# An attention and gMLP kernel whose planner hands the VectorE/GpSimd port to the engine that waits, with squares pushed to GpSimd, part of a layer norm offered to ScalarE, and the last stores on two queues

## Chip, cores, metric

One core of one Trainium2 chip. The metric is device microseconds (us) of one execution. A run reads about 1.8 us more than the span from the first to the last instruction in its trace, so spans are compared with spans and times with times. Single executions of this kernel scatter by a few us (291.0 to 296.7 for the kernel before), which is why differences under about 1% are told with an interval.

Engine names in the profile: PE is TensorE's matmul, PEld its weight load, DVE is VectorE, ACT is ScalarE, POOL is GpSimd, SP is SyncE (the q behind a name is its DMA queue). L441 is line 441 of that kernel; lines shift between kernels, so L418 of before is L441 of after.

## The reference

```python
def rmsnorm(x, g):
    rms = np.sqrt(np.mean(x * x, axis=-1, keepdims=True) + 1e-06)
    return x / rms * g
q_n, k_n = rmsnorm(q, g_q), rmsnorm(k, g_k)          # q, k, v: 8 x 12 x 448 x 64
scores = 1 / 8 * np.matmul(q_n, k_n.transpose(0, 1, 3, 2))
attn = softmax(scores); x = attn @ v                 # then heads side by side: 8 x 448 x 768

h = np.maximum(x @ w_in, 0.0)                        # 768 -> 1024
u, v = h[..., :512], h[..., 512:]
v_n = (v - mean(v)) / np.sqrt(var(v) + 1e-06)        # the layer norm of the change
v_s = einsum('ts,bsd->btd', w_spatial, v_n) + b_spatial[None, :, None]
out = (u * v_s) @ w_out                              # 8 x 448 x 768
```

The heads are worked off in 24 groups of 4 (three groups for each of the 8 batch entries). "Group 2 ended" means that the first batch entry's attention is complete; from then on its unit (the gMLP part) can start.

## The kernel before

The program is not written in the order in which it runs. Each piece of work is a `Task` with the engines that may do it and what each would cost; a `Planner` simulates the engines while the kernel is built, and emits each instruction at the place that this simulation gives it. The chip gets the resulting instruction lists, one for each engine. Between the lists there are semaphores for data and for buffers only.

VectorE and GpSimd share one port pair into the on-chip memory SBUF (the prediction names the page of the Trainium skill and a case in this trace: a GpSimd scaling of 2.58 us in place of 1.69). The planner models it with `locked`, a time up to which the port is taken:

```python
    def start_of(self, t, e, free):
        at = max(free[e], t.after)
        if e == "POOL" or (e == "DVE" and t.port):
            at = max(at, self.locked)          # wait for the port, in the plan
        ...
    def run(self, fill=None):
        ...                                    # pick the task that can start first
            t.emit(e)
            free[e] = at + occ
            t.done = at + lat
            if (e == "POOL" and t.dma == 0) or (e == "DVE" and t.port):
                self.locked = at + occ         # the port is taken, in the plan
```

The tasks that matter (cut):

```python
    # squares of q and k: 128x896 f32
    costs = {"POOL": (1.65, 1.75)}
    if early:                                  # the first 8 groups
        costs = {"POOL": (1.65, 1.75), "ACT": (0.86, 1.0), "DVE": (1.0, 1.13)}
    a = add(f"square{i} G{G}", costs, d - (8 if early else 19) + 0.1 * i, emit, port=True, ...)
    # scaling of q and k by 1/rms: 128x896, two SBUF inputs
    costs = {"POOL": (1.65, 1.75)}
    if early:
        costs = {"POOL": (1.65, 1.75), "DVE": (1.0, 1.13)}
    a = add(f"scaled{i} G{G}", costs, ..., port=True, deps=[rs], ...)
    # layer norm, applied on VectorE
    dve.tensor_scalar(out=vn.t[0:n, c, :], in0=vs.t[0:n, c, :], scalar1=mv.t[0:n, c, 0:1],
                      scalar2=rv.t[0:n, 1, c:c + 1], op0=ALU.subtract, op1=ALU.mult)
    # loads of v and of the weights are issued by GpSimd, those of q and k and the stores by SyncE
    pool.dma_start(out=w_out, in_=moe_w_out.rearrange("(c p) m -> p c m", p=128))
    for y in range(2):
        sync.dma_start(out=o[2 * c + y], in_=ob.t[64 * y:64 * y + 64, :])
```

Of the kernel before, what the change touches and what calls it, by code (L numbers as in the profile page):

```python
# [44 lines left out]
class Task:  # L45
    def __init__(self, name, costs, pos, emit, deps=(), get=(), use=(), mode=None, dma=0.0, after=0.0,
                 port=False):
        self.name, self.costs, self.pos, self.emit = name, costs, pos, emit
        self.deps = [d for d in deps if d is not None]
        self.get = list(get)  # L50
        self.held = list(use)
        self.use = self.get + self.held
        for b in self.use:
            b.left += 1
        self.mode = mode
        self.dma = dma
        self.after = after
        self.port = port
        self.done = None


class Planner:
# [4 lines left out]
    LOOK = {"PE": 0.15, "ACT": 0.1, "DVE": 0.1, "POOL": 0.2, "SP": 0.2}  # L67

    def __init__(self, trace=None):
        self.tasks = []  # L70
        self.trace = trace

    def add(self, *a, **k):
        t = Task(*a, **k)
        self.tasks.append(t)
        return t

    def start_of(self, t, e, free):
        at = max(free[e], t.after)
        if e == "POOL" or (e == "DVE" and t.port):  # L80
            at = max(at, self.locked)
        for d in t.deps:
            if d.done is None:
                return None
            at = max(at, d.done)
        if any(b.slot is None for b in t.held):
            return None
        need = {}
        for b in t.get:
            if b.pool.ordered and b.seq != b.pool.taken + need.get(b.pool, 0):  # L90
                return None
            need[b.pool] = need.get(b.pool, 0) + 1
        for p, n in need.items():
            f = sorted(p.free)
            if f[n - 1] == math.inf:
                return None
            at = max(at, f[n - 1])
        return at

    def run(self, fill=None):  # L100
        free = {"PE": 0.0, "ACT": 0.0, "DVE": 0.0, "POOL": 0.0, "SP": 0.0}
        mode, dma = None, 0.0
        self.locked = 0.0
        left = list(self.tasks)
        while left:
            ready = {}
            for t in left:
                for e in t.costs:
                    at = self.start_of(t, e, free)
                    if at is not None:  # L110
                        ready.setdefault(e, []).append((at, t))
            best = None
            for e, c in ready.items():
                end = {}
                first = min(at for at, _ in c)
                for at, t in c:
                    if at > first + self.LOOK[e]:
                        continue
                    if len(t.costs) > 1:
                        mine = at + t.costs[e][1]  # L120
                        other = min(
                            (self.start_of(t, o, free) + t.costs[o][1] for o in t.costs if o != e))
                        if other < mine - 1e-6:
                            continue
                    s = t.pos
                    if e == "PE" and t.mode != mode:
                        s += 0.6
                    key = (s, at)
                    if best_e_is(end, key):
                        end["k"], end["t"], end["at"] = key, t, at  # L130
                if "t" in end and (best is None or end["at"] < best[0]):
                    best = (end["at"], e, end["t"])
            at, e, t = best
            occ, lat = t.costs[e]
            if e == "PE" and t.mode != mode:
                sw = 0.095
                occ, lat = occ + sw, lat + sw
                mode = t.mode
            if e == "PE" and fill is not None:
                fill(free["PE"], at)  # L140
# [6 lines left out]
            free[e] = at + occ  # L147
            t.done = at + lat
            if (e == "POOL" and t.dma == 0) or (e == "DVE" and t.port):
                self.locked = at + occ  # L150
            if t.dma:
                dma = max(dma, at + occ + 1.6) + t.dma
                t.done = dma + 1.3
# [5 lines left out]
            if self.trace is not None:  # L159
                self.trace.append((at, at + occ, t.done, e, t.name))  # L160
            left.remove(t)


def best_e_is(end, key):
    return "k" not in end or key < end["k"]
# [11 lines left out]
def kernel(  # L177
# [49 lines left out]
    P_rv = Pool(many(2, [128, 2, 4], FP, "rv"))  # L227
# [11 lines left out]
    plan = Planner(TRACE)  # L239
# [33 lines left out]
    def fill(a, b):  # L273
        if b < 25.5 and b - a > 0.6:
            dummies(int((b - max(a, 2.0) - 0.4) / 0.11))


    def due(G, r=0.0):
        x = G + r / 7.0
        return 12.0 + (6.3 * x if x < 3 else 18.9 + 9.8 * (x - 3))  # L280
# [6 lines left out]
    for G in range(NGT):  # L287
        b, g = divmod(G, NG)
        for i in range(2):
            bf = raw[G, i] = Buf(P_raw[i])  # L290

            def emit(e, bf=bf, src=(q_x, k_x)[i][b][g]):
                sync.dma_start(out=bf.t, in_=src)

            raw_t[G, i] = add(f"load{i} G{G}", {"SP": (0.6, 0)}, due(G) - 26 + i * 0.1, emit, get=[bf], dma=1.4,
                              after=0.0 if G < 3 else due(G) - 26)

# [3 lines left out]
    g_t = add("g", {"SP": (1.2, 0)}, due(0) - 25.8, emit, dma=0.1)  # L301
# [7 lines left out]
    g_t = add("g2", {"DVE": (0.3, 0.3)}, due(0) - 2.5, emit, deps=[g_t])  # L309
# [4 lines left out]
    g_t = add("g2 col", {"PE": (0.1, 0.4)}, due(0) - 2.5, emit, deps=[g_t], get=[g_b], mode="G")  # L314
# [3 lines left out]
    g_t = add("g2 copy", {"DVE": (0.1, 0.2)}, due(0) - 2.5, emit, deps=[g_t], use=[g_b])  # L318
# [65 lines left out]
    for G in range(NGT):  # L384
        early = G < EARLY
        d = due(G)
        ms_b = Buf(P_st)
        red = []
        for i in range(2):
            sqb = Buf(P_sq)  # L390

            def emit(e, i=i, sqb=sqb, r=raw[G, i]):
                if e == "ACT":
                    act.activation(out=sqb.t, in_=r.t, func=AF.Square, bias=0.0, scale=1.0)
                else:
                    eng_of[e].tensor_tensor(out=sqb.t, in0=r.t, in1=r.t, op=ALU.mult)  # L396
            costs = {"POOL": (1.65, 1.75)}
            if early:
                costs = {"POOL": (1.65, 1.75), "ACT": (0.86, 1.0), "DVE": (1.0, 1.13)}
            a = add(f"square{i} G{G}", costs, d - (8 if early else 19) + 0.1 * i, emit, port=True,  # L400
                    deps=[raw_t[G, i]], get=[sqb], use=[raw[G, i]])

            def emit(e, i=i, sqb=sqb, ms=ms_b):
                dve.tensor_reduce(out=ms.t[:, i], in_=sqb.t.rearrange("p a (s d) -> p (a s) d", d=D),  # L404
                                  axis=AX.X, op=ALU.add)
            red.append(add(f"reduce{i} G{G}", {"DVE": (1.0, 1.13)}, d - (7 if early else 17) + 0.1 * i, emit,
                           deps=[a], get=[ms_b] if i == 0 else [], use=[sqb] + ([ms_b] if i else [])))
# [6 lines left out]
        for i in range(2):  # L414
# [14 lines left out]
            if G < PE_TURNED:  # L429
# [10 lines left out]
                def emit(e, i=i, bf=bf, tb=tb):  # L440
                    ps = bf.t.bitcast(BF)[:, 0:NS * 128]  # L441
                    o = tb.t.rearrange("p s j -> p (s j)")
                    if i == 0:
# [3 lines left out]
                parts.append((add(f"turned{i} G{G}", {"DVE": (0.54 + 0.06 * i, 0.68 + 0.06 * i)}, d - 1.5 + 0.1 * i, emit,  # L447
# [110 lines left out]
    for b in range(B):  # L558
# [37 lines left out]
        lr = add(f"ln_rstd b{b}", {"ACT": (0.5, 0.65)}, pos, emit, deps=st, get=[rv], use=[mv])  # L596
        vns = []
        for c in range(4):
            n = 128 if c < 3 else 64

            def emit(e, c=c, n=n, vs=vs, mv=mv, rv=rv, vn=vn):
                dve.tensor_scalar(out=vn.t[0:n, c, :], in0=vs.t[0:n, c, :],
                                  scalar1=mv.t[0:n, c, 0:1], scalar2=rv.t[0:n, 1, c:c + 1],
                                  op0=ALU.subtract, op1=ALU.mult)
            vns.append(add(f"ln_apply{c} b{b}", {"DVE": (0.33, 0.42)}, pos + 0.1, emit, port=True, deps=[lr],
                           get=[vn] if c == 0 else [], use=[vs, mv, rv] + ([vn] if c else [])))
# [38 lines left out]
        for c in range(3):  # L645
# [18 lines left out]
            def emit(e, ob=ob, c=c, o=out_s):  # L664
                for y in range(2):
                    sync.dma_start(out=o[2 * c + y], in_=ob.t[64 * y:64 * y + 64, :])
            add(f"store{c} b{b}", {"SP": (0.9, 0)}, pos + 1, emit, deps=cs, use=[ob], dma=1.4)
# [16 lines left out]
        def emit(e, ob=ob, o=out_s):  # L684
            for h in range(2):
                sync.dma_start(out=o[6][:, 384 * h:384 * h + 384], in_=ob.t[64 * h:64 * h + 64, 0:384])
        add(f"store3 b{b}", {"SP": (0.9, 0)}, pos + 1, emit, deps=[a], use=[ob], dma=0.7)

    plan.run(fill)


TRACE = None
# [30 lines left out]
```

## Time and profile before

| | before |
|---|---|
| time, median of the first 3 runs (range) | 296.38 us (291.02 to 296.69) |
| span of the profiled run, granted clock | 293.3 us, 0.984 |
| busy: TensorE / ScalarE / VectorE / GpSimd | 272.7 / 232.5 / 199.1 / 144.0 us |
| TensorE idle in the whole span (293.3 - 272.7) | 20.6 us |
| first score matmul / values of group 2 ended / first unit matmul | 13.35 / 39.82 / 40.26 us |

TensorE is busy 93% of the span, so what counts is where its 20.6 idle us lie. The list of waits of TensorE (what it waited for, us in total, times, longest) names them; these are the rows that the argument needs:

```profile
PE pss L480 <- ACT et L503: 5.7, 12, 1.0
PE ps L435 <- DVE nq L418: 2.0, 2, 1.6
PE ps L435 <- DVE nk L418: 1.2, 2, 0.7
```

TensorE hardly waits for a scaled key (nk): 1.2 us, twice. The groups of VectorE by form, with shapes, count, busy us and mean ns, show the instructions that take the shared port:

```profile
L418 DVE TENSOR_TENSOR nk<-kf,rs 128x896 bf16<-128x896 f32 x7 | 8.7, 1247 | 0.0
L418 DVE TENSOR_TENSOR nq<-qf,rs 128x896 bf16<-128x896 f32 x6 | 7.6, 1270 | 0.8 <-ACT rs L411 0.8
L602 DVE TENSOR_SCALAR vn<-vs,mv,rv 128x512 bf16<-128x512 bf16 x24 | 10.9, 508 | 1.8 <-ACT rv L595 1.8
```

A scaling lasts 1.08 us when GpSimd leaves the port free (the prediction shows two), so the mean of 1.25 has a little waiting in it. That is the column to watch.

### The profile page before, as it was taken

How to read it: one execution, taken by the hardware profiler on the slowest of the kernel's cores; microseconds unless marked ns; L12 is line 12 of the kernel's file. 1: busy time of each engine (PE TensorE's matmuls, PEld its weight loads, DVE VectorE, ACT ScalarE, POOL GpSimd, SP SyncE). 2: the span in 40 equal slices, each digit the busy share in tenths (PEclk: the TensorE clock that was granted, in tenths of full speed). 3: DMA queues.
4: the chain of work that ended last, by engine and by line, in shares of the span. 5: the costliest groups of instructions: out<-in, count | busy, mean ns of one | idle time of the engine just before them, and what ended most of it. 6: DMA issues, size and time to landing. Idle time of an engine off the chain costs nothing.

```text
span 293.3 us, 6975 instructions
## 1 busy us (share of the span) xinstructions
PE 272.7 (93%) x2812; PEld 121.6 (41%) x2823; DVE 199.1 (68%) x324; ACT 232.5 (79%) x372; POOL 144.0 (49%) x121
## 2 busy tenths in 40 slices
PE   6568899998999999999999999999999999999992
PEld 6433335443444343443434443434444433444441
DVE  3999889777677776957776758758677437452630
ACT  4799896887988786879977988978989987775532
POOL 8172017209494988289992699277965000000000
PEclk9999898999999999999999999999999999999998
DMA  7999998194999958996999679976995370004206
GB/s 238 318 291 241 297 227 106 31 209 91 188 240 260 163 122 213 272 212 188 212 182 223 206 161 176 217 201 190 236 202 57 75 191 2 0 2 121 70 0 189
DMA packets 65451, 50.02 MB, mean 171 GB/s; under 512 B 41929, under 2 KB 61898, under 8 KB 65418
## 3 DMA queue, kind: packets, MB, share of 16 engines
q1 hardware_dynamic: 51594, 41.30, 58.0%
q0 software_dynamic: 13824, 8.27, 20.2%
q8 instruction: 22, 0.36, 0.5%
q14 instruction: 11, 0.09, 0.1%
HBM read 38.55 MB, written 11.01 MB: 169 GB/s over the span
## 4 chain that ended last, share of the span: by engine, by line
PE 65%; DMA 9%; DVE 7%; issue 6%; ACT 5%; POOL 3%; SPq 3%; POOLq 0%; DVEq 0%; ACTq 0%
PE ps L576 11%; PE ps L654 10%; PE pss L480 10%; PE ps L614 10%; PE ps L539 9%; PE ps L630 6%; PE ps L521 5%; DMA qf<-in_q_dram 4%; DMA kf<-in_k_dram 4%; ACT et L503 3%; PE ps L675 2%; DVE nk L418 1%; DVE nq L418 1%; POOL sq L396 1%; DVE ms L404 1%
## 5 line engine op out<-in xcount | busy, mean ns | idle before, releaser
L503 ACT ACTIVATE et<-pss 128x896 bf16<-128x896 f32 x168 | 144.0, 914 | 11.7 <-PE pss L480 11.6
L404 DVE TENSOR_REDUCE ms<-sq 128x14 f32<-128x896 f32 x48 | 51.4, 1078 | 10.4 <-POOL sq L396 5.8
L480 PE MATMUL pss<-qT,kT 64*64 64x448 bf16 x672 | 51.8, 366 | 6.7 <-ACT et L503 5.7
L418 POOL TENSOR_TENSOR nq<-qf,rs 128x896 bf16<-128x896 f32 x18 | 30.5, 1692 | 39.1 <-ACT rs L411 28.5
L576 PE MATMUL ps<-w_in,xt 128*128 128x512 bf16 x181 | 45.6, 387 | 0.7 <-issue 0.2
L539 PE MATMUL ps<-et,vt 128*32 128x448 bf16 x768 | 40.8, 354 | 0.0
L418 POOL TENSOR_TENSOR nk<-kf,rs 128x896 bf16<-128x896 f32 x17 | 29.9, 1761 | 21.3 <-ACT rs L411 21.3
L614 PE MATMUL ps<-xt,w_in 128*128 128x448 bf16 x192 | 39.8, 354 | 0.0
L654 PE MATMUL ps<-w_out,gt 128*128 128x384 bf16 x192 | 36.4, 328 | 1.9 <-DVE gt L635 1.9
L546 DVE TENSOR_TENSOR xt<-ps,rc 128x448 bf16<-128x448 f32 x48 | 28.9, 619 | 13.4 <-PE ps L539 7.3
L396 POOL TENSOR_TENSOR sq<-qf 128x896 f32<-128x896 f32 x17 | 29.4, 1731 | 10.7 <-DMA qf<-in_q_dram 8.9
L396 POOL TENSOR_TENSOR sq<-kf 128x896 f32<-128x896 f32 x17 | 28.7, 1689 | 11.7 <-DMA kf<-in_k_dram 7.4
L480 PEld LDWEIGHTS <-kT 64*64 64x64 bf16 x672 | 14.9, 105 | 38.1 <-issue 35.1
L588 DVE BATCH_NORM_STATS2 s<-vs 128x6 f32<-128x512 bf16 (+1 forms) x32 | 22.0, 689 | 12.7 <-ACT vs L554 12.4
L635 DVE TENSOR_TENSOR gt<-ps,us 128x448 bf16<-128x448 f32 x32 | 19.6, 621 | 13.0 <-PE ps L630 9.9
L576 PEld LDWEIGHTS <-xt 128*128 128x128 bf16 x192 | 17.3, 99 | 25.8 <-issue 8.4
L630 PE MATMUL ps<-w_spT,vn 128*128 128x448 bf16 (+1 forms) x128 | 27.9, 354 | 0.0
L539 PEld LDWEIGHTS <-vt 128*32 128x32 bf16 x768 | 18.5, 97 | 20.1 <-issue 8.1
L644 DVE COPY osb<-ps 128x384 f32<-128x384 f32 x28 | 15.3, 555 | 16.8 <-PE ps L654 12.2
L614 PEld LDWEIGHTS <-w_in 128*128 128x128 bf16 x192 | 17.2, 98 | 20.8 <-issue 6.7
L654 PEld LDWEIGHTS <-gt 128*128 128x128 bf16 x192 | 16.7, 98 | 20.2 <-issue 7.2
L521 PE MATMUL ps<-et,ones 128*32 128x448 bf16 x384 | 23.3, 364 | 0.0
(64 smaller groups left out, 264.8 us busy)
## 6 DMA issues: line engine op xcount, KB each, us to landing
qf<-in_q_dram SPq DMA_DIRECT2D x24, 448.0 KB, 6.0
kf<-in_k_dram SPq DMA_DIRECT2D x24, 448.0 KB, 7.1
out_dram<-osb SPq DMA_DIRECT2D x48, 192.0 KB, 3.0
vt<-in_v_dram POOLq DMA_DIRECT2D x16, 192.0 KB, 8.8
vt<-in_v_dram POOLq DMA_DIRECT2D x16, 144.0 KB, 7.9
w_in<-in_moe_w_in_dram POOLq DMA_DIRECT2D x2, 768.0 KB, 13.6
out_dram<-osb SPq DMA_DIRECT2D x16, 96.0 KB, 2.7
w_out<-in_moe_w_out_dram POOLq DMA_DIRECT2D x1, 768.0 KB, 23.5
```

The source lines that it names most:

```text
L396: eng_of[e].tensor_tensor(out=sqb.t, in0=r.t, in1=r.t, op=ALU.mult)
L404: dve.tensor_reduce(out=ms.t[:, i], in_=sqb.t.rearrange("p a (s d) -> p (a s) d", d=D), axis=AX.X, op=ALU.add)
L418: eng_of[e].tensor_tensor(out=nb.t.rearrange("p s a d -> p a s d"), in0=r.t.rearrange("p a (s d) -> p a s d", d=D), in1=P_rs[G % 4][:, i]. ...
L480: pe.matmul(out=ps[64 * h:64 * h + 64, a, 0:S], lhsT=kb[64 * a:64 * a + 64, slot, 64 * xk:64 * xk + 64], rhs=qb[64 * a:64 * a + 64, :, 64 ...
L503: act.activation(out=eb.t[:, r], in_=bf.t[:, :, 0:S], func=AF.Exp, bias=0.0, scale=1.0)
L521: pe.matmul(out=bf.t[32 * l:32 * l + 32, 0:S], lhsT=ones[:, (0 if c < 3 else 1 + x), :], rhs=eb.t[:, r, a, :], start=(c == 0), stop=(c == ...
L539: pe.matmul(out=bf.t[32 * l:32 * l + 32, 0:S], lhsT=vb.t[:, 2 * (g + 3 * a) + x, c, half::2], rhs=eb.t[:, r, a, :], start=(c == 0), stop=( ...
L546: dve.tensor_tensor(out=xb.t[:, j * S:j * S + S], in0=bf.t[:, 0:S], in1=rc.t, op=ALU.mult)
L576: pe.matmul(out=bf.t, lhsT=xb.t[:, j * S + 128 * c:j * S + 128 * c + 128], rhs=w_in[:, j, DH:DF], start=(j == 0), stop=(j == 5))
L614: pe.matmul(out=bf.t[:, 0:S], lhsT=w_in[:, j, 128 * f:128 * f + 128], rhs=xb.t[:, j * S:j * S + S], start=(j == 0), stop=(j == 5))
L630: pe.matmul(out=bf.t[:, 0:S], lhsT=vn.t[0:kp, c, 128 * f:128 * f + 128], rhs=w_spT[0:kp, c, :], start=(c == 0), stop=(c == 3))
L654: pe.matmul(out=bf.t[:, 0:384], lhsT=gt.t[:, f, 128 * c:128 * c + 128], rhs=w_out[:, f, 384 * h:384 * h + 384], start=(f == 0), stop=(f == 3))
```

## The change

Its intent: start the first group sooner, let the planner look further ahead and wait for urgent work, take squares away from the busy ScalarE, let ScalarE do some of the layer norm instead, and shorten the tail. The diff, cut to its core:

```diff
-    LOOK = {"PE": 0.15, "ACT": 0.1, "DVE": 0.1, "POOL": 0.2, "SP": 0.2}
+    LOOK = {"PE": 0.3, "ACT": 0.9, "DVE": 1.1, "POOL": 0.6, "SP": 0.2}
+    WAIT = 4.0
...
-                    s = t.pos
+                    s = t.pos + self.WAIT * (at - first)
...
-                if "t" in end and (best is None or end["at"] < best[0]):
+                if top is not None and (best is None or top[2] < best[0]
+                                        or (top[2] == best[0] and best[1] == self.holder)):
                     best = ...                 # a tie for the port goes to the engine that did not hold it
...
             if (e == "POOL" and t.dma == 0) or (e == "DVE" and t.port):
-                self.locked = at + occ
+                self.locked, self.holder = at + occ, e
...
-        d = due(G)
+        d = due(G) - (3.0 if G == 0 else 0.0)
+   squares:           bias={"ACT": 0.5 if G == 1 else 5.0, "DVE": 4.0} if G else None
+   evictions of the first groups: "ACT": (0.8, 0.95) allowed beside VectorE
...
+            dve.scalar_tensor_tensor(out=rv.t[:, 2, :], in0=mv.t[:, :, 0], scalar=-1.0, in1=rv.t[:, 1, :],
+                                     op0=ALU.mult, op1=ALU.mult)               # shift = -mean/std
+                if e == "ACT":
+                    act.activation(out=vn.t[0:n, c, :], in_=vs.t[0:n, c, :], func=AF.Identity,
+                                   bias=rv.t[0:n, 2, c:c + 1], scale=rv.t[0:n, 1, c:c + 1])
...
-                    sync.dma_start(out=o[2 * c + y], in_=ob.t[64 * y:64 * y + 64, :])
+                    (pool if y and b == B - 1 else sync).dma_start(out=o[2 * c + y], in_=ob.t[64 * y:64 * y + 64, :])
...
+NUDGE = {"exp G4 r2": -9, "rstd G3": -6, ...}   # 186 single shifts of priority
```

## The prediction

> **What bounds the kernel now.** I read the busy table by stretch first, because a share over the whole span hides that this kernel has a ramp, a steady part and a tail. Columns: the stretch, its length, then busy time and instruction count of TensorE's matmuls, its weight loads, VectorE, ScalarE and GpSimd, then the granted clock, the DMA share and GB/s.
>
> ```profile
> 10.00:20.00 10.00, 6.31 (x85) 4.15 (x85) 9.97 (x12) 8.66 (x14) 4.90 (x5) 1.00 1.20 301
> 20.00:30.00 10.00, 8.22 (x117) 4.00 (x117) 10.00 (x13) 9.40 (x14) 3.64 (x6) 0.90 1.07 248
> 30.00:40.00 10.00, 8.93 (x149) 4.09 (x141) 8.53 (x11) 8.59 (x15) 0.00 (x0) 0.93 1.22 285
> ...
> 120.00:140.00 20.00, 19.78 (x208) 8.21 (x204) 14.33 (x26) 17.30 (x28) 13.43 (x9) 1.00 0.99 217
> ...
> 240.00:260.00 20.00, 20.00 (x207) 7.98 (x206) 11.07 (x22) 15.62 (x25) 0.00 (x0) 1.00 0.03 7
> ...
> 280.00:293.30 13.30, 7.73 (x48) 3.90 (x45) 2.50 (x4) 3.85 (x8) 0.00 (x0) 0.91 0.38 104
> ```
>
> The steady part is TensorE's: from 60 to 280 us the twelve stretches add up to 216.3 us of matmul in 220, so only 3.7 us are idle there, and no re-ordering of other engines can give more than that back. Its work is the same after the change. In the ramp TensorE is not the bound: 6.3 and 8.2 us of 10, part of it dummy matmuls that only keep the clock up. VectorE is, at 9.97 and 10.00 us of 10, with ScalarE next to it, while GpSimd does 4.9, 3.6 and then nothing. From 30 us the rows themselves say that a third engine is free: GpSimd's timeline has one hole.
>
> ```profile
> 22.80 0.84 POOL L354 DMA_DIRECT2D w_out<-in_moe_w_out_dram  x1
> 43.08 2.58 POOL L418 TENSOR_TENSOR nk<-kf,rs 128x896 bf16<-128x896 f32 x1 [19.43 <-ACT rs L411]
> ```
>
> After 23.6 us it stands still for 19.4 us, because the planner of before gives early squares and scalings to whichever engine ends them first. Next I read the timeline up to the first score matmul.
>
> ```profile
> 7.10 0.95 ACT L394 ACTIVATE sq<-qf 128x896 f32<-128x896 f32 x1 [0.70 <-DMA qf<-in_q_dram]
> 7.96 0.30 ACT L410 ACTIVATE lnms<-ms,eps 128x28 f32<-128x28 f32 x1
> 8.09 1.09 DVE L404 TENSOR_REDUCE ms<-sq 128x14 f32<-128x896 f32 x1 [0.50 <-ACT sq L394]
> 9.09 1.08 DVE L418 TENSOR_TENSOR nq<-qf,rs 128x896 bf16<-128x896 f32 x1
> 10.09 1.09 DVE L418 TENSOR_TENSOR nk<-kf,rs 128x896 bf16<-128x896 f32 x1
> ...
> 11.23 0.56 PE L435 MATMUL ps<-ident,nk 128*128 128x128 bf16 x7 [0.44 <-DVE nk L418]
> 11.62 1.08 DVE L404 TENSOR_REDUCE ms<-sq 128x14 f32<-128x896 f32 x1
> 12.62 0.68 DVE L446 TENSOR_SCALAR kT<-ps,g_col 128x896 bf16<-128x896 bf16 x1
> 13.35 0.57 PE L480 MATMUL pss<-qT,kT 64*64 64x448 bf16 x8 [0.94 <-DVE kT L446]
> ```
>
> The sums of squares of the first group end at 7.52. Its Ln waits until 7.96 behind a square of the second group on ScalarE; its scaling, ready at 8.52, waits until 9.09 behind a reduce of the second group on VectorE; and the key eviction, whose transposes end at 11.79, waits until 12.62 behind another such reduce. Each is work of lower urgency that got in first, 0.44 + 0.57 + 0.83 = 1.84 us. Last, the tail:
>
> ```profile
> 283.67 3.20 PEld L654 LDWEIGHTS <-gt 128*128 128x128 bf16 x21 [0.67 <-DVE gt L635]
> 285.21 4.01 SPq L666 DMA_DIRECT2D out_dram<-osb  x6
> 288.07 0.49 ACT L642 ACTIVATE osb<-ps 128x384 f32<-128x384 f32 x1 [0.28 <-PE ps L675]
> 289.32 1.19 SPq L686 DMA_DIRECT2D out_dram<-osb  x2
> ```
>
> The last copy ends at 288.56, but the SyncE queue is still issuing the three earlier row blocks (six issues in 4.01 us from 285.21), so the last two issues go out from 289.32 on and end at 290.51; the span ends at 293.3. Just before, TensorE waits 0.67 us for the last gate on VectorE.
>
> **What the Trainium skill says.** (1) "SBUF — State Buffer", section "Who interferes with whom": VectorE and GpSimd share one port pair under an exclusive lock, an instruction with two SBUF inputs or in a two-port mode takes part, and a reduce or an operand in PSUM does not. The trace agrees: the first GpSimd scaling above took 2.58 us beside a 1.09 us VectorE scaling that started 0.06 us earlier, against 1.69 when alone. So moving squares and scalings from VectorE to GpSimd removes its contention partner as well; what is left on VectorE in the ramp (reduces of 1.08, evictions from PSUM) does not take the lock. (2) "ScalarE: Activation LUTs", section "What ACT_TABLE_LOAD costs": an activation costs 186 ns plus 0.833 ns per column, and each per-partition pointer operand adds about 93 ns. The trace agrees: the key scaling of 896 columns with one pointer took 1043 ns (1025 by the rule), the 512-column relu without one 598 (613). The new scaling on ScalarE has two, so I estimate 186 + 186 + 427 = 799 ns, where the planner's function for ScalarE reckons 478 of occupation. (3) Same page, section "Table sets: the hidden batching unit": identity is in every set, so Identity beside Exp and Ln should load no table; the trace has one load at the start though Copy and Relu are used, which fits. (4) "DMA: Bandwidth & Descriptors", section "Issuing engines are not separate DMA queues": a second issuing engine saves sequencer time only. Before's stores take 582 ns of issue in the median and land after 3.0 us, so only issue time is to be had.
>
> **The change part by part.** *First scores.* The priority of the first group is moved 3 us forward, engines may now look about 1 us ahead and wait for a more urgent task at a price, and both evictions may go to ScalarE. I expect the 1.84 us of inversions mostly gone: first score at about 11.6, gain 1.7.
>
> *Ramp.* From the first score at 13.35 to the end of the values of group 2 at 39.83 there are 26.5 us for three groups, 8.8 each. ScalarE's own share of a group is 7 exponentials started 0.81 apart (5.7), Ln and Exp of the reciprocal (1.05 started to started) and of the norm (0.49): 7.2, so 21.7 for three, if it were the bound and did nothing else. VectorE's load per group is two reduces (2.1), two scalings (2.1), two evictions (1.3), two products of 0.62: 6.7, plus squares. With scalings and squares on GpSimd it falls to about 4.6, and GpSimd takes 4 x 1.69 = 6.8 per group, which fits but leaves it nearly full together with 8.2 us of descriptor work, so some scalings stay on VectorE. Of 4.8 us between 26.5 and 21.7 I book 3.0. From there TensorE is the bound, so an earlier start of the unit's matmuls (40.26 now) reaches the end one to one. ScalarE loses most of its 11 squares of 0.95 us: those at 40, 46 and 47 us stand where TensorE waits for exponentials. Half-clock stretches (3.4 us from 28.0 and from 48.5 in the record) cost up to 1.7 each; lower gap limits for dummies may spare the first, and I book 0.5.
>
> *Layer norm.* Eight small VectorE instructions of some 0.2 us (the like-sized aggregate takes 0.18) are added between the norm's Exp and the scaling, about 0.25 us more on a chain that ends beside the u matmuls. In the last batch the scalings end at 278.86 and the spatial matmuls start at 279.68: the slack of 0.8 hides it. Scalings on VectorE average 508 ns for 128 partitions, with lock waits in them; if 12 of 32 go to ScalarE, that is 9.6 us there, as much as the squares free. Neutral, minus 0.3 for under-priced tasks delaying exponentials.
>
> *Steady part.* Of 3.7 us idle, the long list of single nudges and the waiting planner may recover 1.5.
>
> *Tail.* With one issue of each pair on either queue, the last store can be issued at 288.6 on SyncE and end its issue 1.3 us earlier (290.51 to 289.2). The GpSimd half costs 0.69 per issue, as the value loads, and may land later; I book 0.9, and 0.3 for the gate.
>
> Sum: 1.7 + 3.0 + 0.5 - 0.3 + 1.5 + 1.2 = 7.6 of the span of 293.3. Runs read 1.8 us above the span (295.06 for the profiled one) and their median is 296.38, with one at 291.02. I put the new median at 288.0, 2.8% below.
>
> **The rivals.** *A: TensorE's steady part takes it back.* If the ramp only moves idle time, because VectorE or ScalarE falls behind while the second and third batch start, the gain is the first score and the tail: 3 us, 293. For it: ScalarE is 8.2 to 8.6 of 10 in 40 to 60 already. Against: from 60 us on there is hardly a wait of TensorE for ScalarE (1.6 us in all). *B: GpSimd becomes the ramp's bound.* A square there takes 1.69 instead of 0.95, two squares and two scalings one after the other 6.8, plus descriptors: then the ramp keeps its 8.8 per group and only tail and first score are gained, 292 to 293. For it: the bias of 4 to 5 us against the other engines is large; against: 19.4 us of empty GpSimd. *C: more than booked.* Both half-clock stretches gone and the ramp wholly ScalarE-bound: 4 to 5 us more, 283. For it: one run of before at 291.02 shows that some 5 us hang on such things.
>
> **Range and chances.** A and B set the upper end: 292.5. C sets the lower: 283. The 2% line is 290.5. The middle sum lies 2.5 us under it, and two independent terms (ramp, steady) must both fail to miss it, but the spread of before's own runs is as large. Faster 0.74, same 0.24, slower 0.02, the last for a planner whose prices are so wrong that exponentials wait.
>
> **What would show it.** First score in the new timeline at 11 to 12 us; GpSimd without a hole over 8 us before 45, and its squares 40 or more of 48, with at most 5 on ScalarE; values of group 2 ended by 35 to 37 and first unit matmuls there; TensorE idle of 60 to 280 at most 3 us; Identity rows near 0.80 us each, no second table load; last issue ended 1 us after the last copy. Wrong if the first unit matmul still starts at about 40 (B), or starts early while TensorE's idle time between 40 and 100 grows by the same amount (A).

## The result, and the profile after

Ratios here are the mean time of one kernel's fast runs over that of the other's of the same rounds, so not quite the ratio of the medians.

The changed kernel is **slower**: median 306.64 us (306.32 to 308.99, 4 runs) against 295.65 (4 runs), ratio 1.048 with a 95% interval of 1.034 to 1.063. All runs are in the fast state. The spans are 304.9 and 293.3 us, the granted clocks 0.963 and 0.984.

Where do the 11.6 us of span come from? TensorE does the same matmuls in both kernels (with 94 dummies, matmuls whose result nothing uses, instead of 96), so I split the span into its busy and its idle time, by stretch, from the busy table:

| stretch, us | idle before | idle after | difference |
|---|---|---|---|
| 0 to 60 | 11.4 | 16.5 | +5.2 |
| 60 to 100 | 1.3 | 4.0 | +2.8 |
| 100 to 280 | 2.4 | 1.9 | -0.5 |
| 280 to the end | 5.6 | 6.8 | +1.2 |
| idle in all | 20.6 | 29.3 | +8.7 |
| busy in all | 272.7 | 275.6 | +2.9 |

So 8.7 us are new waits, most of them before 100 us, and 2.9 us are the same matmuls taking longer. TensorE's waits after:

```profile
PE ps L458 <- DVE nk L441: 9.1, 3, 4.9
PE pss L506 <- ACT et L529: 5.1, 12, 0.8
PE ps L665 <- DVE vn L637: 3.7, 3, 2.0
```

The waits for exponentials (et) hardly changed. The new ones are for scaled keys (nk), 9.1 us in three waits, and for the scaled layer norm (vn), 3.7 in three. Both come from VectorE instructions that take the shared port. The forms show that they have become slow, not many:

```profile
L441 DVE TENSOR_TENSOR nk<-kf,rs 128x896 bf16<-128x896 f32 x6 | 17.2, 2861 | 1.3 <-ACT rs L434 1.2
L441 DVE TENSOR_TENSOR nq<-qf,rs 128x896 bf16<-128x896 f32 x4 | 5.4, 1360 | 0.0
L637 DVE TENSOR_SCALAR vn<-vs,rv 128x512 bf16<-128x512 bf16 x19 | 11.0, 620 | 0.3
L625 DVE SCALAR_TENSOR_TENSOR rv<-mv,rv 128x4 f32<-128x4 f32 x8 | 4.5, 562 | 1.5 <-ACT rv L621 1.2
```

Ten scalings are left on VectorE (13 before), and together they last 22.6 us, where ten times 1.08 would be 10.8: 11.8 us of waiting inside the instructions, against 2.3 in the 13 of before (16.3 less 14.0). Of these, 9.0 us sit in two of them (4.67 and 6.44 us long). This is the timeline around the second (start, duration, engine, line, operation; in brackets the idle time of the engine ahead of it and what ended it):

```profile
39.03 0.83 POOL L369 DMA_DIRECT2D w_out<-in_moe_w_out_dram  x1
...
39.36 6.44 DVE L441 TENSOR_TENSOR nk<-kf,rs 128x896 bf16<-128x896 f32 x1
...
39.87 1.70 POOL L414 TENSOR_TENSOR sq<-kf 128x896 f32<-128x896 f32 x1
...
41.51 1.69 POOL L441 TENSOR_TENSOR nq<-qf,rs 128x896 bf16<-128x896 f32 x1
43.16 1.68 POOL L414 TENSOR_TENSOR sq<-qf 128x896 f32<-128x896 f32 x1
...
45.85 0.93 PE L458 MATMUL ps<-ident,nk 128*128 128x128 bf16 x7 [4.90 <-DVE nk L441]
...
47.35 0.92 ACT L529 ACTIVATE et<-pss 128x896 bf16<-128x896 f32 x1 [6.71 <-PE pss L506]
```

The key scaling starts on VectorE at 39.36, while GpSimd is issuing the load of w_out. Three GpSimd instructions start after it, and all three finish before it: it ends at 45.80, 0.96 us after the last of them (43.16 + 1.68 = 44.84). So the port was not given to the one that came first, and it was not given at the next change of GpSimd's instruction either. TensorE stands still for 4.90 us, then needs 0.93 us for seven transposes that took 0.56 in before, because its clock has dropped; ScalarE's exponentials stand still for 6.71 us. The first such scaling, with one line ahead that is two issues of 0.64 us, merged:

```profile
15.39 1.29 POOL L358 DMA_DIRECT2D w_in<-in_moe_w_in_dram  x2
16.69 1.70 POOL L414 TENSOR_TENSOR sq<-qf 128x896 f32<-128x896 f32 x1
18.34 1.69 POOL L414 TENSOR_TENSOR sq<-kf 128x896 f32<-128x896 f32 x1
```

```profile
16.32 4.67 DVE L441 TENSOR_TENSOR nk<-kf,rs 128x896 bf16<-128x896 f32 x1
```

Again the scaling arrives inside a descriptor issue and ends 0.96 us after GpSimd's last instruction of the run (20.99 against 20.03). In the rows by stretch, with the columns that the prediction explains, the two cost this (starved: the instruction has started, but waits for the port while GpSimd runs others):

```profile
10.00:20.00 10.00, 5.37 (x67) 3.40 (x67) 9.89 (x9) 6.19 (x9) 7.90 (x6) 0.97 1.20 301
20.00:30.00 10.00, 8.36 (x95) 3.60 (x96) 9.32 (x11) 5.84 (x10) 5.41 (x7) 0.69 1.06 252
...
40.00:50.00 10.00, 5.10 (x44) 1.91 (x33) 9.48 (x6) 2.34 (x4) 5.21 (x4) 0.66 0.78 182
...
60.00:80.00 20.00, 17.72 (x168) 7.98 (x166) 16.48 (x22) 12.19 (x20) 13.53 (x11) 0.91 0.59 77
```

Between 40 and 50 us VectorE looks busy (9.48 of 10), but with six instructions; it is waiting, and a busy column alone would have hidden that. The granted clock falls to 0.69 and 0.66 in the stretches with a starved scaling. The Trainium skill, page "TensorE: Matmul & The Clock Gate", Part 1 on the clock gate, says that TensorE drops to half rate after an idle window of about 3.4 us and needs a busy one to return. The trace agrees on the lengths: its clock record shows half-clock stretches (a granted clock of 0.5) of 6.8, 6.8, 3.4 and 3.4 us from 19.4, 43.3, 67.2 and 87.7, 20.5 us in all, against two of 3.4 in before (and one at the tail in each). It differs on how much idle time is needed: the clock fell 2.1 us into TensorE's wait at 19.4 and 2.3 us into that at 43.3. The stretch at 67.2 follows two slow layer-norm scalings (1.77 us, behind the issues of v loads, and 2.46 us, behind such an issue and a square) and TensorE's wait of 2.0 us for vn; the one at 87.7 follows three waits for exponentials, the longest of 0.8 us. So shorter waits are enough; how much idle time it takes is not shown.

### The profile page after: what moved, and what is told of

Its sections match the earlier page's. It is cut to its first block, busy times and chain, and to the rows that moved or that the text cites. A ratio compares the mean times of both kernels' runs of the same rounds, so it can differ in the third digit from the quotient of the medians.

```text
span 304.9 us, 6998 instructions
## 1 busy us (share of the span) xinstructions
PE 275.6 (90%) x2821; PEld 124.8 (41%) x2821; DVE 217.0 (71%) x335; ACT 224.1 (73%) x356; POOL 168.9 (55%) x138
## 4 chain that ended last, share of the span: by engine, by line
PE 48%; issue 24%; DVE 11%; POOL 7%; ACT 6%; DMA 1%; POOLq 0%; SPq 0%; DVEq 0%
PE ps L602 9%; PE pss L506 9%; PE ps L565 7%; PE ps L649 5%; PE ps L689 5%; PE ps L665 5%; PE ps L547 4%; ACT et L529 4%; DVE nk L441 4%; POOL sq L414 3%; DVE vn L637 3%; POOL nq L441 2%; POOL nk L441 2%; DMA kf<-in_k_dram 1%; PE ps L458 1%
## 5 line engine op out<-in xcount | busy, mean ns | idle before, releaser
L529 ACT ACTIVATE et<-pss 128x896 bf16<-128x896 f32 x168 | 144.3, 914 | 33.2 <-PE pss L506 32.6
L426 DVE TENSOR_REDUCE ms<-sq 128x14 f32<-128x896 f32 x48 | 50.7, 1074 | 8.5 <-POOL sq L414 4.5
L441 POOL TENSOR_TENSOR nq<-qf,rs 128x896 bf16<-128x896 f32 x20 | 34.9, 1746 | 38.9 <-ACT rs L434 34.3
L414 POOL TENSOR_TENSOR sq<-qf 128x896 f32<-128x896 f32 x22 | 38.8, 1763 | 14.5 <-DMA qf<-in_q_dram 7.1
L602 PE MATMUL ps<-w_in,xt 128*128 128x512 bf16 x192 | 46.4, 387 | 0.0
L414 POOL TENSOR_TENSOR sq<-kf 128x896 f32<-128x896 f32 x22 | 37.1, 1688 | 13.2 <-DVE ms L426 12.1
L565 PE MATMUL ps<-et,vt 128*32 128x448 bf16 x768 | 42.7, 361 | 0.0
L689 PE MATMUL ps<-w_out,gt 128*128 128x384 bf16 x192 | 35.5, 327 | 0.6 <-DVE gt L670 0.5
L665 PE MATMUL ps<-w_spT,vn 128*128 128x448 bf16 (+1 forms) x128 | 29.4, 365 | 4.0 <-DVE vn L637 3.7
L701 POOL DMA_DIRECT2D out_dram<-osb x3 | 1.7, 557 | 50.7 <-ACT osb L677 50.6
L670 DVE TENSOR_TENSOR gt<-ps,us 128x448 bf16<-128x448 f32 x32 | 19.6, 620 | 13.1 <-PE ps L665 11.8
L547 PE MATMUL ps<-et,ones 128*32 128x448 bf16 x384 | 24.1, 373 | 0.0
```

The lines of the kernel that those rows point to most:

```text
L414: eng_of[e].tensor_tensor(out=sqb.t[:, h], in0=r.t[:, h], in1=r.t[:, h], op=ALU.mult)
L426: dve.tensor_reduce(out=ms.t[:, i, h], in_=sqb.t[:, h].rearrange("p a (s d) -> p a s d", d=D), axis=AX.X, op=ALU.add)
L441: eng_of[e].tensor_tensor(out=nb.t.rearrange("p s a d -> p a s d"), in0=r.t.rearrange("p a (s d) -> p a s d", d=D), in1=P_rs[G % 4][:, i]. ...
L529: act.activation(out=eb.t[:, r], in_=bf.t[:, :, 0:S], func=AF.Exp, bias=0.0, scale=1.0)
L547: pe.matmul(out=bf.t[32 * l:32 * l + 32, 0:S], lhsT=ones[:, (0 if c < 3 else 1 + x), :], rhs=eb.t[:, r, a, :], start=(c == 0), stop=(c == ...
L565: pe.matmul(out=bf.t[32 * l:32 * l + 32, 0:S], lhsT=vb.t[:, 2 * (g + 3 * a) + x, c, half::2], rhs=eb.t[:, r, a, :], start=(c == 0), stop=( ...
```

## The experiments

The theory: **the changed planner orders the VectorE port instruction ahead of GpSimd's next ones, but only in the plan. Nothing on the chip makes GpSimd wait, and with 44 squares on it (34 before) its runs of ready work are long, so an instruction that loses the port loses it for the whole run.** The rivals: the squares on GpSimd are simply too slow (1.69 us against 0.95 on ScalarE), the layer-norm part costs the time, the stores cost it, or the nudges are at fault. I ran twelve kernels in three calls; each call has its own chip and its own runs of before.

The edit that enforces the plan, used in several of them, is this (shortened; below, a + line in words stands for an edit that is told and not printed):

```diff
+            NOTED[0] = None
             t.emit(e)                          # each emit notes the instruction it made
+            if e == "DVE" and t.port:
+                self.handed = NOTED[0]
+            elif e == "POOL" and NOTED[0] is not None and t.dma == 0:
+                if self.handed is not None:    # GpSimd waits for the VectorE instruction planned ahead of it
+                    tc.add_manual_dep(NOTED[0].ins, self.handed.ins.name, DependencyInfo(Sync, DATA), reason="port")
+                self.handed = None
```

It moves no instruction on any engine; it only adds semaphore waits to GpSimd's squares and scalings.

### x1: two waits only

```diff
+   the wait above, only where the handed task is "scaled1 G1" or "scaled1 G4" (the two starved scalings)
```

> The changed kernel with two waits added: GpSimd's instruction that the plan puts behind the key scalings of groups 1 and 4 on VectorE now waits for them; every engine's order is as it was. Theory (GpSimd keeps the shared port from one instruction to the next, so a VectorE scaling that the plan slots between two of them starves): the two scalings fall from 4.67 and 6.44 us to under 2, TensorE's wait for the scaled keys from 9.1 us to under 2, the half-clock stretches that follow the idle time get fewer, and the time falls by 8 to 12 us, to 295 to 298. Rival (the order of the changed plan is worse in itself; the starved scalings are a symptom off the path): the time falls by less than 3 us, to over 303.

Measured: 301.09 us median, ratio to before 1.022 (1.015 to 1.028). So two waits in a program of some 7,000 instructions take back about half of the loss, less than the theory expected and more than the rival. TensorE's waits for nk fell from 9.1 to 1.9 us. The rest moved: another key scaling, at 19.5, now lasts 4.16 us, and the waits for vn grew from 3.7 to 4.9 us. The half-clock stretches did not get fewer, as the theory had them: six of 3.4 us (in the profiled run, the slowest of the four), 20.5 us in all, as much as in the kernel after. The two scalings are a cause, and not the only place of it.

### x2: every GpSimd instruction waits, DMA issues too

```diff
-            elif e == "POOL" and NOTED[0] is not None and t.dma == 0:
+            elif e == "POOL" and NOTED[0] is not None:
```

> The changed kernel with the planned handover enforced everywhere: each GpSimd instruction that the plan puts behind a VectorE instruction with a claim on the port waits for it. Theory: all the excess of VectorE's port instructions (11.8 us in the scalings, 6.2 in the layer norm's, 4.2 in the key scale, 3.2 in the new shift) falls to under 6 in sum, and the time is 2 to 4 us below the run with two waits, 291 to 295, about the kernel before. Rival (waiting costs GpSimd as much as VectorE gains, and GpSimd's later squares hold up others): same as with two waits within 1 us, or slower.

Measured: 297.86, ratio 1.006 (0.999 to 1.013), no longer told from before, though above the 291 to 295 that were expected. The waits for nk and vn are gone from the top of TensorE's list, and another took their place:

```profile
PE ps L575 <- DMA vt<-in_v_dram: 6.0, 2, 4.9
```

Holding back a DMA issue delays a load: the values' operand came late. So the waits are right for the tensor work and wrong for the issues.

### x3: the two-queue stores alone, on before

```diff
-                    sync.dma_start(out=o[2 * c + y], in_=ob.t[64 * y:64 * y + 64, :])
+                    (pool if y and b == B - 1 else sync).dma_start(out=o[2 * c + y], in_=ob.t[64 * y:64 * y + 64, :])
```

(and the same for the last, shorter pair)

> The kernel before with the last batch's stores alone on two queues. Prediction's step: the last issue ends about 1.3 us earlier and the span is 0.9 us shorter, 0.3%. Rival (the software queue's half lands later and eats it): no difference beyond 0.2 us after the last copy, or longer. To be read from the profile's tail, from the last copy's end to the end of the span (4.7 us in the kernel before), since whole runs scatter by 2%.

Measured: 295.96, ratio 1.000 (0.994 to 1.006). The last issues:

```profile
289.01 0.58 SPq L686 DMA_DIRECT2D out_dram<-osb  x1
```

```profile
289.27 0.53 POOL L686 DMA_DIRECT2D out_dram<-osb  x1 [0.24 <-ACT osb L642]
```

The last copy ends at 288.98 and the last issue at 289.80, 0.8 us later, where before took 1.9 (288.56 to 290.51). The issue time was saved as hoped, and yet the time from the last copy to the end of the span grew from 4.7 to 5.9 us. Before's last store landed at 292.30, 1.0 us ahead of the end; here it landed at 292.52, 2.4 us ahead of the end. So the program's closing took some 1.4 us longer, and a store issued by GpSimd also takes longer to land:

```profile
out_dram<-osb POOLq DMA_DIRECT2D x3, 192.0 KB, 3.5
```

against 3.0 for SyncE's in before. The kernel after shows the same closing (last landing 302.42, end 304.9). I see in the trace that GpSimd's last steps follow SyncE's by about 1.1 us; why, I did not test.

### x4: the port measured by itself

A program with no attention in it and a wrong result on purpose. ScalarE opens each of 18 scenes; GpSimd runs three squares, without a DMA issue, with one ahead of the first, or with one ahead of the second; VectorE runs a short reduce that sets its arrival, then one port instruction.

```python
for dma_at in (None, 0, 1):
    for what in ("TT", "TS"):        # scaling with two SBUF inputs; tensor_scalar of 512 bf16
        for delay in (64, 192, 448): # columns of the reduce
            scene(what, dma_at, delay)
```

> A probe with a wrong result on purpose: 18 scenes, in each three GpSimd squares of the kernel's shape back to back, without a DMA issue, with one ahead of the first square, or ahead of the second; and one VectorE instruction that arrives 0.2 to 0.6 us later: the two-input scaling or the one-input bf16 scaling. Theory: GpSimd keeps the port as long as its next instruction is ready, so both kinds last until GpSimd's run ends (up to 5 us) in at least some scenes. Rival 1: the port goes to whoever has waited longest, so the VectorE instruction ends after one square, 1.7 to 2.8 us at most, and the long ones in the kernel have another cause. Rival 2: only an arrival during the descriptor work of a DMA starves, since both long ones of the kernel arrived in one: long in the scenes with a DMA ahead of the first square alone.

Measured (one execution): the outcome depends on what GpSimd was doing at the arrival. Without a DMA issue the scaling lasted 2.1 to 2.5 us: it got the port after the running square, one change of instruction later, and so it did with the issue ahead of the second square. With the issue ahead of the first and the arrival inside it:

```profile
62.72 0.80 POOL L67 DMA_DIRECT2D w_d<-in_moe_w_out_dram  x1 [4.70 <-ACT gate L59]
62.99 6.46 DVE L74 TENSOR_TENSOR tt_o<-f_in,rs 128x896 bf16<-128x896 f32 x1
63.55 4.95 POOL L69 TENSOR_TENSOR sq<-f_in 128x896 f32<-128x896 f32 x3
```

The scaling started 0.56 us ahead of the first square and waited for all three of them (63.55 + 4.95 = 68.50; it ended at 69.45). This is the 39.36 case again, in a program where nothing else runs. The tensor_scalar did the same (5.66 us for 0.40 alone), and arrivals at the very start of the issue were served at once. So rival 2 came true, and the theory was too broad: in these scenes an instruction loses the port for GpSimd's whole run only when it arrives in the descriptor work of an issue; otherwise it loses it for one instruction.

### x8: the arrival swept

```diff
+    for d in range(60, 3400, 240): scene("TT", None, d)   # arrivals over the first squares, no DMA
+    for d in range(40, 900, 66):   scene("TT", 0, d)      # arrivals over the descriptor work
```

> A second probe, wrong result on purpose: the two-input scaling alone, its arrival swept over two back-to-back squares in steps of 0.25 us, then over the descriptor work of a DMA with three squares behind it in steps of 0.07 us. From the first probe: an arrival inside a square is served after that square (1.7 us after its start at most plus its own 1.08), an arrival more than some 0.3 us into the descriptor work is served only after all three squares, one within 0.1 us of its start at once. Expected: a switch point between 0.1 and 0.36 us into the descriptor work, and all later arrivals in it starve; among the squares, starvation only for an arrival within about 0.1 us of a change from one square to the next, as in the run with two waits. Rival: the starvation comes from the start of the scene, not from the DMA, and then some arrivals inside squares starve too.

Measured (one execution), without a DMA issue: all 14 arrivals were served after the square that was running, 1.1 to 2.5 us. With one: the four scalings that started before the issue or up to 0.05 us into it lasted 1.08 us. The other ten, nine from 0.12 us into the issue on and the last 0.10 us into the square behind it, lasted 6.61 down to 5.80, each ending 0.95 to 0.96 us after the third square. The two sides of the switch:

```profile
112.22 0.80 POOL L67 DMA_DIRECT2D w_d<-in_moe_w_out_dram  x1 [1.65 <-ACT gate L59]
112.27 1.08 DVE L80 TENSOR_TENSOR tt_o<-f_in,rs 128x896 bf16<-128x896 f32 x1
...
119.68 0.80 POOL L67 DMA_DIRECT2D w_d<-in_moe_w_out_dram  x1 [1.52 <-ACT gate L59]
119.80 6.61 DVE L80 TENSOR_TENSOR tt_o<-f_in,rs 128x896 bf16<-128x896 f32 x1
120.50 4.95 POOL L69 TENSOR_TENSOR sq<-f_in 128x896 f32<-128x896 f32 x3
```

So 0.07 us in the arrival decides between nothing and 5.5 us, for work that follows on GpSimd without a gap. One thing did not reproduce: x1's 4.16 us at 19.5 began 0.12 us into the second of three squares behind a DMA issue, and no arrival of the sweep near a change from one square to the next starved. In the kernel after, the layer-norm scaling of 2.46 us, which started in an issue, was served after one square although another followed. These cases are open.

### x5: waits for squares and scalings only

```diff
+   the wait edit as printed above, on after
```

> As the run with all waits, but GpSimd's DMA issues do not wait for VectorE any more, only its squares and scalings do. In the run with all waits TensorE waited 6.0 us for late value loads, and 10.2 us at half clock followed. Theory (the port explains the whole loss, and the DMA issues' waits cost what is left): no wait of TensorE for value loads over 1 us, no more starved scalings than with all waits, 292 to 295, that is the kernel before or up to 1% under it. Rival (the changed plan has nothing left over the old one even with an honest port): within 1% of the run with all waits, 296 to 299.

Measured: 290.69 (289.70 to 291.86), ratio 0.990 (0.986 to 0.994): the same instructions in the same order as the kernel after, now 1% **under** before instead of 4.8% over it, and better than the 292 to 295 expected. The span is 290.1. The key scalings and the layer norm are nearly back to their own durations (1.08 and 0.40 us alone):

```profile
L451 DVE TENSOR_TENSOR nk<-kf,rs 128x896 bf16<-128x896 f32 x6 | 7.3, 1211 | 1.3 <-ACT rs L444 1.2
...
L647 DVE TENSOR_SCALAR vn<-vs,rv 128x512 bf16<-128x512 bf16 x19 | 7.0, 409 | 0.3
```

2861 ns fell to 1211 and 620 to 409. The waits for the port thus account for the whole of the loss. Two things were left: the new shifts still average 560 ns (the longest, 1.87 us, started in the issue of a v load), and TensorE still waited 2.3 us for one v load, where at most 1 us was expected. The run does not yet say what the changed plan is worth.

### x6: the bias on squares alone, on before

```diff
+                    bias={"ACT": 0.5 if G == 1 else 5.0, "DVE": 4.0} if G else None,   # squares kept off ScalarE
```

> The kernel before with the squares' bias alone (off ScalarE and VectorE after group 0). Theory: more GpSimd work back to back in the ramp means more starved VectorE scalings, and the time rises by 2 to 8 us, to 297 to 303. Rival (the prediction's: freed ScalarE and VectorE start the unit's matmuls earlier): the time falls by 2 us or more.

Measured: 309.27, ratio 1.051 (1.045 to 1.057). This one argument (with the terms of the planner that read it) reproduces the loss, and a little more, under the old planner; 297 to 303 were expected. TensorE's waits:

```profile
PE ps L437 <- DVE nk L420: 5.7, 4, 2.2
PE ps L632 <- DVE vn L604: 4.6, 2, 3.5
```

and VectorE's layer-norm scalings average 897 ns in place of 508:

```profile
L604 DVE TENSOR_SCALAR vn<-vs,mv,rv 128x512 bf16<-128x512 bf16 x24 | 20.4, 897 | 1.1 <-ACT rv L597 1.1
```

The trace of x6 agrees with the probes: the five longest port instructions on VectorE (2.8 to 7.1 us) all started inside a DMA issue of GpSimd, and the longest, at 98.41, waited for four GpSimd instructions behind that issue. So the new tie rule of the planner is not needed for the loss; the old planner also counts on a port order that nothing enforces. With squares on GpSimd its lists simply get into each other's way more often.

### x11: the same with the waits

```diff
+   x6 and the wait edit
```

> The squares' part alone on the kernel before (x6, 309 us) with the waits of x5. Theory: it falls by 10 us or more, to 294 to 299, as the changed kernel did, since the port is all that makes this part slow. Rival (GpSimd squares of 1.69 us in the ramp are too slow in themselves, my rival B): it stays over 303.

Measured: 293.17, ratio 0.996 (0.990 to 1.001). The waits take 16 us off x6 (which ran on another chip) and leave it level with before. The layer norm's 897 ns fell to 419:

```profile
L614 DVE TENSOR_SCALAR vn<-vs,mv,rv 128x512 bf16<-128x512 bf16 x24 | 8.9, 419 | 1.2 <-ACT rv L607 1.1
```

### x9: before with the waits, nothing else

```diff
+   before and the wait edit; the plan is before's, instruction for instruction
```

> The kernel before, its order as it is, with the waits of x5: GpSimd's squares and scalings wait for the VectorE port instruction planned ahead of them. Theory: the old plan slots few VectorE instructions between GpSimd's (8.7 us of excess in all, none over 2.3 us), so there is little to gain: 0 to 1% faster, 291 to 294. Rival (the waits are what makes x5 faster than the kernel before, and the changed plan gives nothing): the same 290.7 as x5 within 0.5 us.

Measured: 291.18 (290.14 to 292.44), ratio 0.988 (0.984 to 0.992): the same gain as x5 within the intervals, without any part of the change, as the rival had it. Its port instructions hardly wait any more:

```profile
L428 DVE TENSOR_TENSOR nk<-kf,rs 128x896 bf16<-128x896 f32 x7 | 7.6, 1083 | 0.0
...
L612 DVE TENSOR_SCALAR vn<-vs,mv,rv 128x512 bf16<-128x512 bf16 x24 | 8.6, 412 | 1.8 <-ACT rv L605 1.8
```

So the gain of x5 over before is the waits' and not the changed plan's, as far as ratios from two chips can be compared.

### x7 and x10: the layer-norm part alone, without and with the waits

```diff
+   the added shift, the Identity form and its ScalarE cost, on before (x7) and on x9 (x10)
```

> The kernel before with the layer norm's part alone: the shift on VectorE and the scaling on either engine. Prediction's step: neutral within 1 us. Rival: the new shift has two inputs in SBUF and waits for the port on the norm's chain (0.56 us mean in the changed kernel, 0.16 alone), so TensorE's wait for the scaled values appears and the time rises by 1 to 3 us.

Measured: 302.14, 295.90, 300.43 and 301.05. Three of the four count as slow and one as fast, the profile fell among the slow ones, and there is no verdict: inconclusive.

> The run before it with the layer norm's part added (shift on VectorE, scaling on either engine), to settle x7, whose runs fell into two groups. Prediction's step: within 1 us of x9. Rival: 1 to 3 us slower than x9, because the shift takes the port (0.56 us mean) and the plan reckons 0.48 for a ScalarE scaling that lasts 0.81.

Measured: 295.31 (291.30 to 298.46), ratio 0.997 (0.990 to 1.003), where x9 in the same rounds has 0.988. The layer-norm part seems to cost some 0.9% here, but the intervals overlap, two of its six runs are slow and the fast ones alone scatter by 4 us, so this is a hint.

### x12: x5 without the nudges

```diff
-NUDGE = {"exp G4 r2": -9, ...}
+NUDGE = {}
```

> x5 with the table of nudges emptied: the same rules of the planner, its own order. The planner's own reckoning of the end is 297.8 against 291.4 with nudges. Theory (with the waits the plan is kept on the chip, so its reckoning carries over): 5 to 7 us slower than x5, 296 to 298. Rival (the nudges matter little): within 2 us of x5.

Measured: 298.21 (294.69 to 301.06), half of the runs slow, ratio of the fast ones 1.001 (0.994 to 1.008). About 1% slower than x5's 0.990 from another chip, where 5 to 7 us (about 2%) were expected: the nudges seem to help the changed plan. Without them it is level with before, and behind before with the same waits (x9). The planner's longer look ahead, its price for waiting and the evictions on ScalarE were not run alone.

### The stages side by side

From the profiled runs (all fast), in us. Squares are counted on ScalarE / VectorE / GpSimd.

| kernel | first score | values of group 2 end | first unit matmul | last copy | span | squares |
|---|---|---|---|---|---|---|
| before | 13.35 | 39.82 | 40.26 | 288.56 | 293.3 | 11 / 3 / 34 |
| after | 11.67 | 40.95 | 47.60 | 298.95 | 304.9 | 4 / 0 / 44 |
| x5, after with waits | 11.72 | 39.12 | 40.05 | 284.07 | 290.1 | 4 / 0 / 44 |
| x6, squares alone | 12.97 | 46.68 | 47.12 | 303.93 | 308.3 | 4 / 0 / 44 |
| x11, squares with waits | 13.07 | 40.86 | 41.30 | 287.13 | 291.5 | 4 / 0 / 44 |
| x9, before with waits | 13.02 | 37.78 | 38.22 | 283.74 | 288.4 | 11 / 3 / 34 |

The three groups of the ramp take 8.8 us each in before, 8.25 in x9, 9.1 in x5 and 9.3 in x11 (values of group 2 less first score, by three). Where the port is enforced, the kernels with squares on GpSimd are the slower ones through the ramp, by about 1 us a group.

## Why the prediction was wrong, point by point

**First score: right.** Booked at 11.6, measured at 11.67, a gain of 1.7 us.

**The side facts: right.** ScalarE keeps 4 squares and GpSimd has 44; GpSimd has no hole over 8 us before 45; the last issue ends 0.82 us after the last copy; there is one table load; and Identity with two pointers costs what the rule cited in the prediction gave (estimate 0.80):

```profile
L634 ACT ACTIVATE vn<-vs,rv 128x512 bf16<-128x512 bf16 x5 | 4.0, 807 | 0.2 <-DVE rv L625 0.2
```

**The step that failed:** "moving squares and scalings from VectorE to GpSimd removes its contention partner as well". It did not. The same text let "some scalings stay on VectorE" and never priced them beside a GpSimd that it had just filled: ten stayed, and waited 11.8 us for the port inside themselves (2.3 before); 25 layer-norm scalings and eight new shifts take the port too. x6, x11, x5 and x9 show that this step is the cause: the bias alone makes the loss (+5.1%), the waits alone undo it in two plans (x11, x5), and before with waits keeps its order and gains 1.2% (x9). The prediction's own line, 2.58 us for 1.69, showed a contention of one instruction; what it had no price for is a whole run of GpSimd instructions served before a scaling that had started in a DMA issue (4.67 and 6.44 us in place of 1.08).

**Ramp, booked +3.0: wrong in sign, and also in size without starvation.** The values of group 2 end 1.1 us later than before, and the first unit matmul 7.34 later. With the port enforced (x5) they end 0.7 us earlier, and the first unit matmul 0.2: the 1.6 us won at the first score are mostly spent again. So rival B, GpSimd as the ramp's bound, holds in part; the prediction dismissed it because GpSimd had 19.4 empty us, but empty time in a trace says nothing about when the work is ready.

**Half-clock, booked +0.5: wrong in sign.** Half-clock stretches went from 6.8 to 20.5 us, and the matmuls took 2.9 us more. The prediction saw a drop of the clock as something to be spared, not as what one long wait brings with it.

**Layer norm, -0.3: undecided.** The mechanism is as told except for two sizes: 7 of 32 scalings went to ScalarE, not 12, and the shift, taken for 0.2 us, averaged 0.56 (0.15 at the shortest, 1.87 at the longest, behind a GpSimd square). Its cost in time is only hinted at by x10.

**Steady part, booked +1.5: wrong.** TensorE's busy time from 60 to 280 fell from 216.3 to 214.1 (x5: 216.8, so 0.5 in place of 1.5). Rival A's size is in this: two starved vn scalings lie between 62 and 67, with 2.8 us of new idle time between 60 and 100, and two more from 167.8 on (1.73 and 1.76 us) cost TensorE 1.7 us. (A small misreading in rival A: ScalarE is busy 8.2 and 8.5 of 10 us in 40 to 60, not 8.6.)

**Tail, booked +1.2: right mechanism, no gain.** The issue time was saved, the closing took it back (x3: ratio 1.000). The 0.3 for the gate may have come: waits for gates fell from 1.9 to 0.5 us in all, but no run isolates it.

**The chances.** 0.02 for slower was kept "for a planner whose prices are so wrong that exponentials wait". The exponentials did wait (ScalarE's idle time for scores rose from 11.6 to 32.6 us), though not through prices. The planner also simulates the end of its own plan: 290.1 for before and 291.4 for after (worked out by running its code). I had that code and could have read it as a warning; a large diff with a stated intent was taken for a gain.

## What to carry to other kernels

An order between two engines that only a plan or a cost model knows is no order on the chip: if a shared port must go to the waiting engine, give the other one a semaphore wait, and leave its DMA issues out of it (1% gained here on an untouched plan, 5% on one that had crowded GpSimd). Before moving work to an idle engine, list the instructions left behind that share a port with it, and look for ones whose duration, not count, grows. Look at the mean duration in the groups by form, since a starved instruction counts as busy.

## What the Trainium skill lacked or had wrong

- "SBUF — State Buffer", section "Who interferes with whom": it says that issue order decides who blocks, and that the second to issue waits until the first finishes. The runs agree for arrivals during a GpSimd square (served right after it, 14 of 14 in x8). They differ for arrivals during the descriptor work of a DMA that GpSimd issues: the VectorE instruction that started 0.56 us ahead of the next square waited for three squares (6.46 us in place of 1.08, x4), and in the kernel after for three instructions (6.44 us). I found this on no page.
- Same page and section, on DMA: it tells of VectorE starving GpSimd's descriptor work, and lacks the opposite direction. In x8 a scaling that started up to 0.05 us into the issue was served at once, one from 0.12 us on waited out the three squares behind it.
- Same page and section: it infers that a tensor_tensor with two SBUF inputs leaves descriptor work alone. The runs agree on the issue itself (0.80 us with a scaling beside it, x8). It lacks what becomes of the tensor_tensor: it then waits for squares that started after it.
- "TensorE: Matmul & The Clock Gate", Part 1: it puts the drop to half rate after an idle window of about 3.4 us. In the kernel after the clock fell 2.1 us into a wait (at 19.4), and at 87.7 after waits of at most 0.8 us.
- "DMA: Bandwidth & Descriptors", section "Issuing engines are not separate DMA queues": that a second issuing engine saves sequencer time only is what x3 shows (last issue 0.8 us after the last copy in place of 1.9). It lacks the price at the end of a program: 2.4 us from the last landing to the end with GpSimd issuing, 1.0 without.
